# Window attention and two feed-forward layers on one core: one key tile for the first groups, a dummy exponential, a late `gcol`, and scores ahead of the preceding values

## The chip, the core and the metric

The kernel runs on one core of a Trainium2 chip. The metric is the device time of one execution in microseconds (us); each kernel is run several times and the median is compared. Lower is better.

The engines work side by side, each through its own list of instructions in order: PE (matmuls, turning by matmul), DVE (vector arithmetic), ACT (functions such as exp and tanh, and copies), POOL (slower vector arithmetic, and some transfers), SP (here it only issues transfers). A semaphore wait holds up the instruction that has it and all behind it on its engine.

## The reference

```python
# _attn_ref: q, k, v of (4, 8, 576, 64), causal, window of 64
scores = scale * np.matmul(q, k.transpose(0, 1, 3, 2))
mask = (rel >= 0) & (rel < window)
scores = np.where(mask, scores, -1000000000.0)
scores = scores - np.max(scores, axis=-1, keepdims=True)
attn = np.exp(scores)
attn = attn / (np.sum(attn, axis=-1, keepdims=True) + 1e-09)
return np.matmul(attn, v).astype(np.float32)
# _moe_ref: 2304 tokens, 512 -> 2048 -> 512
h = x @ w_in
g = h * (1.0 / (1.0 + np.exp(-1.702 * h)))
return (g @ w_out).astype(np.float32)
# _moe2_ref: 2304 tokens, 512 -> 1536 -> 512
rms = np.sqrt(np.mean(x * x, axis=-1, keepdims=True) + 1e-06)
xn = x / rms * rms_g
g = xn @ w_gate
silu = g * (1.0 / (1.0 + np.exp(-g)))
val = xn @ w_val
return (silu * val @ w_out).astype(np.float32)
```

The attention's output, as 2304 tokens of 512 values, is the input of the first feed-forward layer, and that layer's output the input of the second.

## The kernel before

**Groups.** The attention is cut into 36 groups of 64 tokens (`W`), all 8 heads of a group together. `attention(g, ...)` does one: scores on PE (into a PSUM bank), row maximum `nm` on DVE, exponentials with their sums `su` on ACT (four instructions a group), the reciprocals `rc` of the sums on DVE, the normalising product `e` by `rc` on POOL, the turning of `e` on PE, a copy of the turned probabilities to `pt` or `pts` on ACT or DVE, the values on PE, and then the result in two parts: `xh` (rounded, by ACT) and `xl` (the rest, by DVE). For the first 8 groups (`NS`) the mask is added by a matmul (`masked_scores`, L432 and L435), and the maximum is taken from PSUM (L440, L442); later groups use `scores`, `masked`, `highest`. From group 18 on (`NPE`) the turning is by DVE and 32 by 32 copies.

**Blocks.** The first layer works on six blocks of 512, 256, 384, 384, 384 and 384 tokens; `a_up` and `a_down` take one of 16 slices of `w_in` and `w_out` each: an up product is 12 matmuls (L554 to L556, three for each of four parts, the second of which reads `xl`), then tanh (L607) and gating (L611) into `th`, a split into `gh` and `gl`, and the down product (L628 to L630). The first block needs groups 0 to 7, the second 8 to 11, the third 12 to 17. The second layer (L912 to L914, L1013 to L1015) follows.

**Weights.** Weights come as 64-bit words of 512 KB for a slice. `w_narrow` loads one into a `raw` buffer (three of them, L336) and makes 32-bit numbers: one ACT step (L340), three DVE steps (L344, L348, L354). `w_split` cuts the number into a high half in a slab (ACT, L312) and a low half (L381, on POOL or DVE). During the first block all 32 slices go through this.

**Order.** Nothing is put in order by hand. Every step is entered with `pl.op(cost, ..., prio)`: costs for each engine that may do it, a priority, and the buffers that it reads, writes and takes. `Planner.emit` plays the steps through with these costs, always the ready one with the lowest priority number first, and the instructions of all engines are written in that order. A changed cost, priority or number of buffers can so move instructions anywhere behind it. `late` adds to the time after which the planner counts a step as finished.

**Start.** `load_q`, `load_k` and `load_v` load 256 KB each through SP. Keys are loaded as two windows at a time and the windows overlap, so each group's load repeats a window of the one before. Buffers: two `q` and four `q0`, two `k` and three `k0`, one `v` and three `v0`. The scores of the first 8 groups take PSUM banks `y0` to `y2` in turn. `gcol` (L1091, L1092) is the second layer's factor `rms_g`, halved; it is first read where the first block's results are scaled (L650, L653). `attention` is called with `step`, the distance by which turning and values come later in priority than scores.

Of the kernel before, what the change touches and what calls it, by code (L numbers as in the profile page):

```python
# [9 lines left out]
F32 = mybir.dt.float32  # L10
# [7 lines left out]
P = 128  # L18
# [188 lines left out]
def window_attention_two_moe_kernel(ctx: ExitStack, tc: tile.TileContext, ins, out):  # L207
# [74 lines left out]
        "q0": (start, 4, [P, NK, 2 * W], F32),  # L282
        "k0": (start, 3, [P, 2, NK, W], F32),
        "v0": (start, 3, [P, DM], F32),
# [7 lines left out]
    pts = at.tile([P, NK, P], F32, name="pts")  # L292

# [37 lines left out]
    def w_narrow(key, src, prio, after=(), apart=False, late=0.0):  # L331
# [25 lines left out]
        got = pl.op({"D": dma(P * 4096)}, fetch, prio - 3, new=[rb], after=after, late=late)  # L357
# [31 lines left out]
    q_of, kw, vw, vals = {}, {}, {}, []  # L389

# [9 lines left out]
    def load_k(g, prio, kind="k"):  # L400
# [3 lines left out]
        t = kw[b, i] = Buf(kind)  # L404
# [14 lines left out]
    def attention(g, p0, step, ekind="e", ptkind="pt", norm=("G",), ptev=("A", "V"), hi=("A",)):  # L419
        q, k, v = q_of.pop(g), kw[wkey(g)], vw[wkey(g)]  # L420
        sb, eb, nb, ub, rb = Buf(f"y{g % 3}" if g < NS else "abank"), Buf(ekind), Buf("nm"), Buf("su"), Buf("rc")
        tb, pb, ob = Buf("bank" if g < NS else "abank"), Buf(ptkind), Buf("abank")
        extra = [START] if ekind == "e0" or ptkind == "pt0" or q.kind == "q0" or k.kind == "k0" or v.kind == "v0" else []

        def scores(e):
            s = make(sb)
            for p in range(NK):
                nc.tensor.matmul(s[:, p * P:(p + 1) * P], q.tile[:, p], k.tile[:, :, p], start=True, stop=True)  # L428

        def masked_scores(e):  # L430
# [3 lines left out]
            for p in range(NK):  # L434
                nc.tensor.matmul(s[:, p * P:(p + 1) * P], q.tile[:, p], k.tile[:, :, p], start=False,  # L435
                                 stop=(p == NK - 1))
# [63 lines left out]
        if g < NS:  # L500
            pl.op({"T": 1.09}, masked_scores, p0, r=[q, k, "mask", "negative", "ident", *extra],
                  w=[("xh", c), ("xl", c), "scores order"], new=[sb])
            pl.op({"V": dve(512) + 0.1}, highest_of, p0, r=[sb], new=[nb])
            pl.op({"A": 4 * act(128, True, 2)}, powers_of, p0, r=[sb, nb, *extra], new=[ub, eb])
        else:
            pl.op({"T": 0.872}, scores, p0, r=[q, k, *extra], w=[("xh", c), ("xl", c), "scores order"], new=[sb, eb],
# [7 lines left out]
        if g < NPE:  # L514
            pl.op({"T": 0.436}, turned, p0 + d, r=[eb, "ident", *extra], w=["turned order"], new=[tb, pb])
# [20 lines left out]
        vals.append(pl.op({"T": 0.872}, values, p0 + d, r=[v, pb, "at", *extra] + (nov if g >= NPE else []), new=[ob]))  # L536
        cost = {"A": act(256, False), "V": dve(256)}
        pl.op({x: cost[x] for x in hi}, x_hi, p0 + d, r=[ob], w=[("xh", c)])
        pl.op({"V": dve(256)}, x_lo, p0 + d, r=[ob, ("xh", c)], w=[("xl", c)])
# [737 lines left out]
```

## Time and profile before

| | |
|---|---|
| median of 3 runs | 926.25 us (926.17 to 926.94) |
| span of the profiled execution | 923.7 us |
| PE busy | 902.2 us, 98% |
| DVE busy | 647.3 us, 70% |
| ACT busy | 438.4 us, 47% |
| POOL busy | 273.2 us, 30% |

The span runs from the first to the last instruction of the profiled execution; its own time with what lies around the span is not listed apart, and the runs' median is 2.55 us above it. Busy times are sums over stages with different limits: in the start no engine is busy throughout, in the first block DVE and PE both nearly are, later PE alone. So the stretches are read one by one, and in each the waits of the engine that is nearly full.

### The profile page before, as it was taken

The numbers are of one execution on the slowest core, as the hardware profiler recorded it, in microseconds if no ns is written. First come the engines' busy times: TensorE is split into PE (matmuls) and PEld (weight loads), VectorE is DVE, ScalarE is ACT, GpSimd is POOL, SyncE is SP. The second block draws the span as 40 slices with busy tenths as digits, with TensorE's granted clock in tenths as the row PEclk, the third lists the DMA queues.
The fourth block names the chain that finished last, engine by engine and source line by source line (L and its number), as shares of the span: only waits on it lengthen the run. The fifth ranks groups of instructions, "written<-read, shape, count | busy, mean of one in ns | idle before, by whom it ended". The sixth has DMA issues, their size and how long they took to land.

```text
span 923.7 us, 15362 instructions
## 1 busy us (share of the span) xinstructions
PE 902.2 (98%) x5436; PEld 835.9 (90%) x5436; DVE 647.3 (70%) x1236; ACT 438.4 (47%) x1081; POOL 273.2 (30%) x387
## 2 busy tenths in 40 slices
PE   8899999999999999999999999999999999999998
PEld 7677789989999999999998989898999999999997
DVE  5999996676767667666467888778667556555553
ACT  6666665566566667565336444443322223322222
POOL 4111012334345342442102622334223225222210
PEclk9999999999999999999999999999999999999999
DMA  8655557665445656543366999888986768966741
GB/s 283 226 174 201 193 188 159 222 206 171 151 147 186 169 183 229 183 160 114 106 231 233 234 359 341 320 280 255 321 236 206 206 201 244 284 205 205 205 144 68
DMA packets 86536, 194.63 MB, mean 211 GB/s; under 512 B 12726, under 2 KB 36027, under 8 KB 84924
## 3 DMA queue, kind: packets, MB, share of 16 engines
q1 hardware_dynamic: 66108, 137.02, 44.5%
q0 software_dynamic: 20352, 56.63, 21.0%
q8 instruction: 43, 0.70, 0.3%
q14 instruction: 33, 0.27, 0.1%
HBM read 140.13 MB, written 53.50 MB: 210 GB/s over the span
## 4 chain that ended last, share of the span: by engine, by line
PE 77%; DVE 12%; DMA 6%; issue 2%; ACT 2%; SPq 0%; POOL 0%; DVEq 0%; ACTq 0%; POOLq 0%
PE bank L912 9%; PE bank L913 9%; PE bank L914 9%; PE y L628 5%; PE y L630 5%; PE y L629 5%; PE bank L554 5%; PE bank L555 5%; PE bank L556 5%; PE y L1013 3%; PE y L1015 3%; PE y L1014 3%; PE abank L428 3%; DVE raw L348 2%; PE abank L487 2%
## 5 line engine op out<-in xcount | busy, mean ns | idle before, releaser
L554 PE MATMUL bank<-xh,slab 128*128 128x384 f32 (+2 forms) x288 | 98.3, 341 | 1.0 <-DVE th L611 1.0
L628 PE MATMUL y<-gh,slab 128*128 128x384 f32 (+2 forms) x288 | 98.5, 342 | 0.5 <-DVE y L653 0.5
L556 PE MATMUL bank<-xh,slab 128*128 128x384 f32 (+2 forms) x288 | 97.0, 337 | 2.0 <-DVE slab L381 2.0
L555 PE MATMUL bank<-xl,slab 128*128 128x384 f32 (+2 forms) x288 | 97.3, 338 | 0.4 <-DVE xl L494 0.3
L630 PE MATMUL y<-gh,slab 128*128 128x384 f32 (+2 forms) x288 | 96.9, 337 | 0.5 <-DVE slab L381 0.5
L629 PE MATMUL y<-gl,slab 128*128 128x384 f32 (+2 forms) x288 | 96.6, 336 | 0.0
L951 ACT ACTIVATE sb<-gh 128x384 f32<-128x384 f32 x72 | 37.8, 525 | 114.0 <-DVE gh L938 114.0
L312 ACT ACTIVATE xh<-sb 128x384 fp32r<-128x384 f32 x72 | 37.1, 521 | 107.5 <-DVE sb L966 107.5
L938 DVE TENSOR_TENSOR gh<-gl,bank 128x384 f32<-128x384 f32 x108 | 59.3, 551 | 35.9 <-PE bank L914 35.1
L611 DVE SCALAR_TENSOR_TENSOR th<-th,bank 128x384 f32<-128x384 f32 (+2 forms) x96 | 52.7, 549 | 42.8 <-ACT th L607 42.3
L913 PE MATMUL bank<-slab,late 128*128 128x384 f32 x228 | 77.0, 338 | 0.0
L913 PE MATMUL bank<-slab,slab 128*128 128x384 f32 x228 | 76.4, 335 | 0.0
L607 ACT ACTIVATE th<-bank 128x384 f32<-128x384 f32 (+2 forms) x96 | 46.7, 486 | 58.1 <-PE bank L556 55.0
L472 POOL TENSOR_TENSOR e<-e,rc 128x512 f32<-128x512 f32 x34 | 37.8, 1111 | 108.9 <-DVE rc L469 102.8
L312 ACT ACTIVATE gh<-th 128x384 fp32r<-128x384 f32 (+2 forms) x96 | 50.2, 523 | 40.3 <-DVE th L611 31.3
L938 DVE TENSOR_TENSOR gl<-gl,bank 128x384 f32<-128x384 f32 x72 | 39.8, 553 | 35.4 <-PE bank L914 31.4
L463 ACT ACTIVATE e<-e,nm 128x128 f32<-128x128 f32 x112 | 43.7, 393 | 33.2 <-DVE nm L458 31.0
L556 PEld LDWEIGHTS bank<-xh,slab 128*128 128x128 f32 x288 | 54.1, 188 | 4.9 <-DVE slab L381 2.8
L554 PEld LDWEIGHTS bank<-xh,slab 128*128 128x128 f32 x288 | 54.1, 188 | 3.6 <-DVE th L611 1.6
L630 PEld LDWEIGHTS y<-gh,slab 128*128 128x128 f32 x288 | 54.1, 188 | 3.2 <-DVE slab L381 1.2
L555 PEld LDWEIGHTS bank<-xl,slab 128*128 128x128 f32 x288 | 54.1, 188 | 3.1 <-DVE xl L494 1.1
L912 PE MATMUL bank<-slab,slab 128*128 128x384 f32 x156 | 53.0, 340 | 3.8 <-ACT th L312 1.7
(198 smaller groups left out, 2596.9 us busy)
## 6 DMA issues: line engine op xcount, KB each, us to landing
slab<-wc POOLq DMA_DIRECT2D x36, 512.0 KB, 4.6
late<-wc POOLq DMA_DIRECT2D x36, 512.0 KB, 4.3
wp<-raw SPq DMA_DIRECT2D x24, 512.0 KB, 4.1
fw<-wp SPq DMA_DIRECT2D x12, 1024.0 KB, 8.1
late<-wo POOLq DMA_DIRECT2D x22, 512.0 KB, 5.5
q<-in_q_dram SPq DMA_DIRECT2D x36, 256.0 KB, 4.4
wc<-slab SPq DMA_DIRECT2D x18, 512.0 KB, 7.1
wc<-late SPq DMA_DIRECT2D x18, 512.0 KB, 5.7
```

The lines of the kernel that those rows point to most:

```text
L312: nc.scalar.activation(out=out, in_=in_, func=AF.Copy)
L554: nc.tensor.matmul(h, w[:, 0, kk], xh_ring[:, kk, cols], start=(kk == 0), stop=False)
L555: nc.tensor.matmul(h, w[:, 0, kk], xl_ring[:, kk, cols], start=False, stop=False)
L556: nc.tensor.matmul(h, w[:, 1, kk], xh_ring[:, kk, cols], start=False, stop=(kk == NK - 1))
L611: nc.vector.scalar_tensor_tensor(out=th, in0=th, scalar=1.0, in1=hb.tile[:, 0:n], op0=ALU.add, op1=ALU.mult)
L628: nc.tensor.matmul(y, s[:, 0, cols], hb.tile[:, 0:n], start=first, stop=False)
L629: nc.tensor.matmul(y, s[:, 0, cols], lb.tile[:, 0:n], start=False, stop=False)
L630: nc.tensor.matmul(y, s[:, 1, cols], hb.tile[:, 0:n], start=False, stop=last)
L912: nc.tensor.matmul(h, w[:, 0, kk], xh[:, kk], start=kk == 0, stop=False)
L913: nc.tensor.matmul(h, w[:, 0, kk], xl[:, kk], start=False, stop=False)
L914: nc.tensor.matmul(h, w[:, 1, kk], xh[:, kk], start=False, stop=kk == 1)
L938: nc.vector.tensor_tensor(out=(make(to) if kind else s.tile)[:, 0:HT].bitcast(F32), in0=s.tile[:, 0:HT].bitcast(F32), in1=b.tile[:, 0:HT], ...
```

## The change

- Keys of the first groups: one tile `k_start` of six windows is filled by three loads of two windows; groups 0 to 5 read it. A group's keys are now a function that gives the tile's part (`k()`), with the list of its load steps beside it (`ktok`), a window pair across two loads having two. The `k0` buffers are gone.
- `q0` has two buffers instead of four, `v0` five instead of three. The loads of the first 8 groups are written as one list with priorities in that order.
- A dummy exponential of one column (`first_exp`) stands first on ACT.
- `gcol` is loaded with priority 1 instead of -20 and scaled with priority 14 instead of 0.
- The first weight's load has a lead of 20.8 instead of 3.0.
- `attention` takes a separate step for the values, `vstep`. For the first 8 groups both stay 0.5; for the later ones turning has 1.7 and values 2.5, where both had 2.
- Costs of scores, turning, values and exponentials in the planner are other numbers.

```diff
-        "q0": (start, 4, [P, NK, 2 * W], F32),
-        "k0": (start, 3, [P, 2, NK, W], F32),
-        "v0": (start, 3, [P, DM], F32),
+        "q0": (start, 2, [P, NK, 2 * W], F32),
+        "v0": (start, 5, [P, DM], F32),
...
+    KS = 6
+    k_start = start.tile([P, KS, NK, W], F32, name="k_start")
...
-        got = pl.op({"D": dma(P * 4096)}, fetch, prio - 3, new=[rb], after=after, late=late)
+        got = pl.op({"D": dma(P * 4096)}, fetch, prio - lead, new=[rb], after=after, late=late)
...
-    def attention(g, p0, step, ekind="e", ptkind="pt", norm=("G",), ptev=("A", "V"), hi=("A",)):
-        q, k, v = q_of.pop(g), kw[wkey(g)], vw[wkey(g)]
+    def attention(g, p0, step, vstep, ekind="e", ptkind="pt", norm=("G",), ptev=("A", "V"), hi=("A",)):
+        q, (k, ktok), v = q_of.pop(g), kw[wkey(g)], vw[wkey(g)]
+        qk = [q, *ktok]
...
-            pl.op({"T": 1.09}, masked_scores, p0, r=[q, k, "mask", "negative", "ident", *extra],
+            pl.op({"T": 1.2}, masked_scores, p0, r=[*qk, "mask", "negative", "ident", *extra],
...
-            pl.op({"A": 4 * act(128, True, 2)}, powers_of, p0, r=[sb, nb, *extra], new=[ub, eb])
+            pl.op({"A": 1.4}, powers_of, p0, r=[sb, nb, *extra], new=[ub, eb])
...
-        vals.append(pl.op({"T": 0.872}, values, p0 + d, r=[v, pb, "at", *extra] + (nov if g >= NPE else []), new=[ob]))
+        vals.append(pl.op({"T": 0.65}, values, p0 + vstep, r=[v, pb, "at", *extra] + (nov if g >= NPE else []), new=[ob]))
...
+    first_exp = start.tile([P, 1], F32, name="first_exp")
     pl.op({"V": 0.2}, lambda e: nc.vector.memset(warm, 0.0), -99, w=["warm"])
+    pl.op({"A": 1.4}, lambda e: nc.scalar.activation(out=first_exp, in_=warm[:, 0:1], func=AF.Exp), -99, r=["warm"])
...
+    for i in range(KS - 1):
+        kw[0, i] = (lambda i=i: k_start[:, i:i + 2]), starts[i // 2:(i + 1) // 2 + 1]
+    loads = [(load_k_start, 0), (load_q, 0, "q0"), (load_q, 1, "q0"), (load_k_start, 2), (load_q, 2), (load_v, 0),
+             (load_q, 3), (load_k_start, 4), (load_q, 4, "q0"), (load_v, 2, "v0"), (load_q, 5, "q0"), (load_k, 6),
+             (load_q, 6), (load_v, 3, "v0"), (load_k, 7), (load_q, 7)]
+    loads += [(load_v, g, "v0") for g in range(4, NS)]
+    for n, (fn, g, *kind) in enumerate(loads):
+        fn(g, n - 95, *kind)
...
-    pl.op({"D": 0.45}, lambda e: nc.sync.dma_start(out=gcol, in_=rms_g), -20, w=["gcol"])
+    pl.op({"D": 0.45}, lambda e: nc.sync.dma_start(out=gcol, in_=rms_g), 1, w=["gcol"], late=6.0)
     pl.op({"V": 0.1}, lambda e: nc.vector.tensor_scalar(out=gcol, in0=gcol, scalar1=0.5, scalar2=None, op0=ALU.mult),
-          0, w=["gcol"])
+          14, w=["gcol"])
...
-        w_narrow(key, src, prio)
+        w_narrow(key, src, prio, lead=3.0 if i else 20.8)
...
-            attention(g, p - 0.3, 2)
+            attention(g, p - 0.3, 1.7, 2.5)
```

How this moves instructions, in three places. Line numbers of the changed kernel are some 4 to 14 higher.

First, DVE where the last of the first 8 groups are under way (`xl` is a group's low part, `pts` and `pt` the copies of turned probabilities, `raw` a weight being narrowed). Before:

```order
L494 TENSOR_TENSOR xl<-abank,xh 128x4x64
L1092 TENSOR_SCALAR gcol<-gcol 128x4
L314 COPY pts<-bank 128x512
L344 TENSOR_SCALAR raw<-raw 128x512
L314 COPY pt_546<-bank 128x512
L348 SCALAR_TENSOR_TENSOR raw<-raw 128x512
```

Now:

```order
L498 TENSOR_TENSOR xl<-abank,xh 128x4x64
L349 SCALAR_TENSOR_TENSOR raw<-raw 128x512
L355 SCALAR_TENSOR_TENSOR raw<-raw 128x512
L472 TENSOR_SCALAR rc<-su 128x4
L473 RECIPROCAL rc<-rc 128x4
L315 COPY pts<-bank 128x512
```

`gcol` no longer stands ahead of the copies; the first weight's steps stand between the `xl` parts.

Second, DVE at the ninth group, behind the reciprocals of its sums; with them POOL starts the normalising product. Before:

```order
L468 TENSOR_SCALAR rc<-su 128x4
L469 RECIPROCAL rc<-rc 128x4
L381 TENSOR_TENSOR slab_86<-raw,slab_86 128x512
L611 SCALAR_TENSOR_TENSOR th<-th,bank 128x512
L381 TENSOR_TENSOR slab_83<-raw,slab_83 128x512
```

Now:

```order
L472 TENSOR_SCALAR rc<-su 128x4
L473 RECIPROCAL rc<-rc 128x4
L615 SCALAR_TENSOR_TENSOR th<-th,bank 128x512 x2
L345 TENSOR_SCALAR raw<-raw 128x512
L573 TENSOR_TENSOR gl<-th,gh 128x512
```

The two low halves of weights behind the reciprocals have gone to POOL, and the gating stands there.

Third, PE where the second block ends and the third begins with `slab_82` (`ident,e` is the turning of a group, `pts,v` the values, `k,q` the scores of the next group, `late_...` the second block's last slices). Before:

```order
L477 MATMUL abank<-ident,e 128x128 x4
L628 MATMUL y_1690<-gh,late_1310 128x256
L629 MATMUL y_1690<-gl,late_1310 128x256
L630 MATMUL y_1690<-gh,late_1310 128x256
L487 MATMUL abank<-pts,v 64x64 x8
L428 MATMUL abank<-k,q 128x128 x4
L554 MATMUL bank<-xh,slab_82 128x384
L555 MATMUL bank<-xl,slab_82 128x384
```

Now:

```order
L634 MATMUL y_1692<-gh,late_1299 128x256
L491 MATMUL abank<-pts,v 64x64 x8
L558 MATMUL bank<-xh,late_1304 128x256
...
L634 MATMUL y_1692<-gh,late_1301 128x256
L432 MATMUL abank<-k,q 128x128 x4
L558 MATMUL bank<-xh,slab_82 128x384
L559 MATMUL bank<-xl,slab_82 128x384
```

The last values of the third block's groups now have an up product and a down product of the second block behind them, ahead of the third block's first product.

## Rows read from the trace of the kernel before

**Rows 1.** The page, busy us, share and instructions of each engine:

```profile
PE 902.2 (98%) x5436; PEld 835.9 (90%) x5436; DVE 647.3 (70%) x1236; ACT 438.4 (47%) x1081; POOL 273.2 (30%) x387
```

**Rows 2.** By stretch: length, busy PE, PEld, DVE, ACT, POOL, clock, DMA share, GB/s:

```profile
5.77:32.00 26.23, 20.78 (x232) 17.49 (x231) 20.16 (x56) 20.42 (x82) 7.42 (x8) 0.93 0.88 292
32.00:150.00 118.00, 114.12 (x629) 92.64 (x630) 110.74 (x197) 75.26 (x161) 18.56 (x16) 1.00 0.55 187
150.00:200.00 50.00, 48.80 (x446) 46.68 (x444) 32.37 (x70) 27.99 (x93) 12.38 (x14) 1.00 0.70 196
```

**Rows 3.** PE's waits, whole span: us in total, times, longest:

```profile
PE abank L487 <- DVE pts L314: 2.8, 1, 2.8
PE bank L556 <- DVE slab L381: 2.0, 2, 1.3
...
PE y L432 <- ACT e L448: 1.1, 1, 1.1
...
PE bank L912 <- DVE th L611: 1.0, 1, 1.0
...
PE y L630 <- DVE slab L381: 0.5, 1, 0.5
```

**Rows 4.** Timeline of ACT at the first group: start, length, instruction, idle before:

```profile
6.75 1.28 ACT L448 ACT_TABLE_LOAD   x1 [6.75 <-DVE nm L442]
8.04 0.37 ACT L448 ACTIVATE e<-y,nm 128x128 f32<-128x128 f32 x1
...
9.43 0.38 ACT L448 ACTIVATE t<-y,nm 128x128 f32<-128x128 f32 x1
```

**Rows 5.** Timeline around `gcol`, all engines:

```profile
17.26 0.44 SPq L1091 DMA_DIRECT2D gcol<-in_rms_g_dram  x1
...
23.50 0.17 DVE L1092 TENSOR_SCALAR gcol<-gcol 128x4 f32<-128x4 f32 x1 [1.54 <-DMA gcol<-in_rms_g_dram]
23.57 0.68 DVE L314 COPY pts<-bank 128x512 f32<-128x512 f32 x1
...
24.31 0.83 PE L487 MATMUL abank<-pts,v 128*64 128x64 f32 x16 [2.79 <-DVE pts L314]
...
25.07 1.12 PE L477 MATMUL bank<-ident,e 128*128 128x128 f32 x4
```

**Rows 6.** Two microseconds after it, by stretch:

```profile
26.00:28.00 2.00, 1.78 (x26) 1.45 (x27) 1.97 (x7) 1.77 (x4) 0.00 (x0) 0.50 0.84 266
```

**Rows 7.** DVE's groups, 5.7 to 32 us: busy, mean ns, idle before:

```profile
L440 DVE TENSOR_REDUCE nm<-y 128x4 f32<-128x512 f32 x8 | 5.5, 683 | 2.5 <-PE y L435 2.4
...
L468 DVE TENSOR_SCALAR rc<-su 128x4 f32<-128x4 f32 x8 | 1.4, 171 | 2.5 <-ACT e L448 1.3 <-ACT t L448 1.0
...
L381 DVE TENSOR_TENSOR slab<-raw,slab 128x512 fp32r<-128x512 f32 x1 | 0.7, 686 | 0.0
```

**Rows 8.** Timeline at the first up product:

```profile
31.58 0.42 DVE L494 TENSOR_TENSOR xl<-abank,xh 128x256 fp32r<-128x256 f32 x1
...
32.06 0.50 PE L555 MATMUL bank<-xl,slab 128*128 128x512 f32 x1 [0.32 <-DVE xl L494]
```

**Rows 9.** Timeline in the first block, POOL, DVE and PE:

```profile
77.13 1.31 POOL L472 TENSOR_TENSOR e<-e,rc 128x512 f32<-128x512 f32 x1 [3.15 <-DVE rc L469]
...
77.46 1.53 DVE L381 TENSOR_TENSOR slab<-raw,slab 128x512 fp32r<-128x512 f32 x1
...
79.04 0.50 PE L556 MATMUL bank<-xh,slab 128*128 128x512 f32 x1 [1.34 <-DVE slab L381]
```

**Rows 10.** Timeline of PE where the third block begins, the four waits:

```profile
191.11 0.38 PE L629 MATMUL y<-gl,late 128*128 128x256 f32 x1 [0.48 <-POOL gl L569]
...
192.56 0.66 PE L477 MATMUL abank<-ident,e 128*128 128x128 f32 x4 [0.26 <-POOL e L472]
...
193.97 0.69 PE L487 MATMUL abank<-pts,v 128*64 128x64 f32 x16 [0.39 <-ACT pts L312]
...
200.78 0.44 PE L554 MATMUL bank<-xh,slab 128*128 128x384 f32 x1 [0.55 <-DVE th L611]
```

More of the change, by code (lines that the diff above doesn't have):

```diff
@@ L329, in window_attention_two_moe_kernel, with w_narrow @@
     w32 = {}
-    def w_narrow(key, src, prio, after=(), apart=False, late=0.0):
+    def w_narrow(key, src, prio, after=(), apart=False, late=0.0, lead=3.0):
         rb = Buf("raw")
@@ L389, in window_attention_two_moe_kernel @@
     q_of, kw, vw, vals = {}, {}, {}, []
+    starts = [("keys", n) for n in range(KS // 2)]
     def wkey(g):
@@ L403, in load_k @@
         b, i = wkey(g)
-        t = kw[b, i] = Buf(kind)
+        t = Buf(kind)
+        kw[b, i] = (lambda: t.tile), [t]
         pl.op({"D": dma(P * 2048)}, lambda e: nc.sync.dma_start(out=make(t), in_=kh[b, :, i:i + 2]), prio, new=[t])
@@ L427, in scores @@
             for p in range(NK):
-                nc.tensor.matmul(s[:, p * P:(p + 1) * P], q.tile[:, p], k.tile[:, :, p], start=True, stop=True)
+                nc.tensor.matmul(s[:, p * P:(p + 1) * P], q.tile[:, p], k()[:, :, p], start=True, stop=True)
         def masked_scores(e):
@@ L434, in masked_scores @@
             for p in range(NK):
-                nc.tensor.matmul(s[:, p * P:(p + 1) * P], q.tile[:, p], k.tile[:, :, p], start=False,
+                nc.tensor.matmul(s[:, p * P:(p + 1) * P], q.tile[:, p], k()[:, :, p], start=False,
                                  stop=(p == NK - 1))
@@ L514, in attention @@
         if g < NPE:
-            pl.op({"T": 0.436}, turned, p0 + d, r=[eb, "ident", *extra], w=["turned order"], new=[tb, pb])
+            pl.op({"T": 0.4}, turned, p0 + d, r=[eb, "ident", *extra], w=["turned order"], new=[tb, pb])
             cost = {"A": act(512, False), "V": dve(512)}
@@ L1081, in window_attention_two_moe_kernel, with load_k_start @@
     pl.op({"G": 0.1}, lambda e: nc.gpsimd.memset(mhalf, -0.5), -97, w=["mhalf"])
[L1083 to L1089 removed]
+    def load_k_start(i, prio):
+        tok = starts[i // 2]
+        pl.op({"D": dma(P * 2048)}, lambda e: nc.sync.dma_start(out=k_start[:, i:i + 2], in_=kh[0, :, i:i + 2]), prio, w=[tok])
+    for i in range(KS - 1):
[6 more added lines that the diff above has]
+        fn(g, n - 95, *kind)
+    for g in range(NS):
+        attention(g, -60 + g, 0.5, 0.5, "e0" if g >= 2 else ("e", "t1")[g], "pt0" if g % 2 else "pt",
                   norm=("G",) if g < NS - 1 else ("V",))
[L1091 removed]
+    pl.op({"D": 0.45}, lambda e: nc.sync.dma_start(out=gcol, in_=rms_g), 1, w=["gcol"], late=6.0)
     pl.op({"V": 0.1}, lambda e: nc.vector.tensor_scalar(out=gcol, in0=gcol, scalar1=0.5, scalar2=None, op0=ALU.mult),
[L1093 removed]
+          14, w=["gcol"])
     pl.op({"V": 0.2}, lambda e: nc.vector.tensor_scalar(out=ones, in0=ident, scalar1=0.0, scalar2=1.0,
```

14 lines of the change are left out of this document (4 added, 10 removed).

## The prediction

> **What bounds the kernel now.** I read the page's busy times first: PE, the matmul engine, is busy for 902 of 923.7 us [rows 1]. So nothing that the change does to other engines counts unless it fills one of PE's gaps, and all gaps together are some 21 us: that is the ceiling, 2.3%. The table by stretch then says where they lie [rows 2]: of the 26.2 us from the first row maximum on DVE (5.77) to the last part of the first token block (32.0), PE works 20.8 and DVE, the vector engine, only 20.2; in the next 118 us, the first block's feed-forward layer, PE is idle for 3.9 and DVE is busy for 110.7 of 118, so these two are nearly balanced there; from 150 to 200 us PE is idle for 1.2. The list of PE's waits names the reasons [rows 3]: one wait of 2.8 us for a copy of turned probabilities, two for a weight's low half (2.0), one for the exponentials (1.1), one for a `th` tile where the second layer begins (1.0).
>
> The three rows that the change aims at are these. ACT, the activation engine, loads its function table at 6.75, 1.28 us long, between the first group's maximum and its first exponential, and then does one group each 1.39 us (8.04 to 9.43) [rows 4]. The dummy exponential asks for the same table at the start, where ACT has nothing to do until 6.75, so it costs nothing itself. DVE stands still for 1.54 us at 23.50, because the scaling of `gcol` waits for a 2 KB transfer that was issued at 17.26 behind the weights; the copy of the turned probabilities is queued behind it, and PE waits 2.79 us for that copy [rows 5]. [...] The first layer's first matmul chain cannot go past its second matmul before the last `xl` part is written: it is issued at 31.58 and the matmul follows at 32.06 after 0.32 of waiting [rows 8]. The time of this last `xl` is therefore the measure of the whole start.
>
> **The change part by part: the start.** DVE writes that last `xl`, and it is the engine to count. Before, it does 20.16 us of work in 26.23, so it is idle for 6.07 [rows 2]. The changed order gives DVE nearly the same list up to the eighth `xl`: one copy of turned probabilities more (0.68 [rows 5], since ACT does one fewer), one low half of a weight less (0.69 [rows 7], it goes to POOL) and no `gcol` (0.17). The work stays at 20.0 us and only idle time can be won. It has four parts [rows 5, 7]: 1.5 for `gcol`; 2.5 before the sums' reciprocals (L468), for ACT; 2.4 before the row maxima, of which 1.4 lie ahead of 5.77; and some 1.0 for the smaller ones. The first goes altogether: `gcol`, which is not read until the first block's results are scaled, is now prepared some twenty-five DVE instructions after the last of the eight `xl`, and its transfer is issued after the loads of the ninth and tenth group, so the copy is no longer behind it. Of the second I take 1.8 (the 1.0 of the second group, whose exponentials start 1.28 us earlier with the table already loaded, and 0.8 of the 1.3 that the other groups wait). Of the waits for the scores I take nothing: the first scores still wait for masks and identity. So 1.5 + 1.8 = 3.3 us.
>
> Bounds for this term: the lower one is the `gcol` wait alone, 1.5; the upper one adds all of L468's 2.5 and 0.5 for matmuls that ran at the low clock (the turning's 1.12 us [rows 5]), 4.5. Whether the clock falls again I cannot exclude: PE still has gaps of about a microsecond between the last groups.
>
> The table load is 1.28 us in the row and the exponential follows at once (8.04) [rows 4]. [...]
>
> The loads. The key tile holds six windows in three transfers, where five were made before, so two transfers of 256 KB fall away in the first eight groups. With five value buffers the values no longer wait for the matmuls of earlier groups, while only two query buffers are left beside the two that stay; the fifth and sixth group's queries wait for the first two groups' scores, which are long done. Ahead of the first weight stand 17 transfers of 256 KB now; with the weight they are 5.0 MB, and at the 292 GB/s of this stretch [rows 2] they need 17 us, so the weight lands at about 19. DVE comes to it at about that time by my count. I cost this at nothing, and at 1 us where it is late; it is inside the lower bound.
>
> **The first block, 32 to 150 us.** The head start is worth something only if it is not used up here. Two things speak for that. Up to the point where the first block's results are scaled, the changed order gives DVE four low halves of weights fewer (0.69 each [rows 7]) and two narrowing steps of a weight of the second layer fewer, together some 3.5 us of 110; the low halves go to POOL, which works for 18.6 of 118 us [rows 2]. And the largest waits there have one cause: POOL normalises a group's probabilities (77.13, 1.31 us), DVE's low half of a weight starts beside it and takes 1.53 instead of 0.69, and PE waits 1.34 [rows 7, 9]. In the order before, such a low half comes right behind or one instruction behind the reciprocals of four groups; in the changed order two of the four have other work there that did not suffer in the trace, and for two (the eleventh and twelfth group) it is the same. I take one of PE's three waits for them as won, the shortest, 0.5 us [rows 3]. Bounds: a gain of 2.5, all three, and a loss of 1.3, one more wait as long as the longest.
>
> [...]
>
> **The later groups, 150 to 200 us and on.** With values at +2.5 and turning at +1.4 instead of both at +1.7 of a plan step, PE's order ahead of the third block changes: before it is turning, a quarter of a down product, values, scores, the new block's first product; now whole products stand between turning, values and scores, and two of the old block's down products come after the new block's first product. PE waits at this place four times: 0.48, 0.26, 0.39, 0.55 [rows 10], together 1.7. With whole products between them, the first three have cover; I take 1.3, bounds 0 and 1.7. Between 200 and 500 us there is nothing of this kind to win: PE is busy throughout. The second layer's matmuls keep their order to the end; the 1.0 at its beginning [rows 3] I leave, with 1.0 either way, since other engines' work is dealt out anew.
>
> **Sum.** 3.3 + 0.5 + 1.3 = 5.1 us off the profiled span of 923.7, so 918.6. The median of the runs, 926.25, lies 2.55 above that span, and I take this as constant: 921.15, said as 921.2.
>
> **The rivals.** First, only `gcol` is won at the start: the exponentials come sooner, but the scores' arrival or the first weight then sets DVE's pace. For it: DVE already waits for scores, 2.4 us [rows 7]. Against it: the fourth group's scores waited for exponentials, not for data [rows 3]. Then 1.5 + 0.5 + 1.3 = 3.3, 922.95: still faster.
>
> Second, the head start is handed back in the first block, because DVE and the weights' buffers set the pace there and not PE. For it: 110.7 of 118 us of DVE work. Against it: PE's 3.9 us of idleness is as small, and DVE has less to do. Only the boundary's 1.3 stays: 924.95, no change.
>
> Third, on the other side: POOL's low halves become the late ones. Ten of the first layer's low halves are on POOL in the changed order and six before, and each is some 0.6 us longer than on DVE. If a product waits 1.3 us for each, as the longest wait for a slab [rows 3], seven of ten cost 9.1; less 3.3 and 1.3 that is 4.5 us slower, 930.75. It decides from the fifth on: four such waits cost 5.2, 0.6 more than the 4.6 won, and five cost 6.5, which is slower by more than 0.2%. Against it: no wait of PE for a slab in the trace names POOL, all name DVE.
>
> Fourth, nearly all upper bounds are met, 4.5 + 2.5 + 1.7 and half of the second layer's 1.0: 9.2 us, 917.0.
>
> **How the numbers follow.** A measurement of this kernel can tell some 0.2%, 1.85 us, from no change: faster is below 924.4, slower above 928.1. Chances: forecast 0.58, first rival 0.13, second 0.14, third 0.09, fourth 0.06. Faster 0.58 + 0.13 + 0.06 = 0.77, same 0.14, slower 0.09. The range must reach the first, second and fourth: 917.0 to 925.2 leaves out the third and about a tenth spread over the ends of the others.
>
> **What would show it.** Right: no idle time of DVE before `gcol`; the table load in the first 3 us; the eighth `xl` at about 28.7 and the first product right behind; PE's waits for a slab at 2 us or less in 32 to 150; no more than 0.5 us of waits where the third block begins. Wrong: a first product later than 30.5 (first rival), PE idle for 6 us or more in the 118 us behind it (second), waits of PE for POOL's slabs (third), or a longer stretch at the low clock than before 28 us.

## The result: one per cent slower, and the profile after

| | before | after |
|---|---|---|
| median of the runs, us | 926.21 (923.99 to 926.94, 6 runs) | 936.20 (933.21 to 938.05, 6 runs) |
| profiled span, us | 923.7 | 933.7 |
| ratio after to before | | 1.010, 95% interval 1.0081 to 1.0119 |

The change makes the kernel 10 us slower. The forecast, 921.2 us with a range of 917.0 to 925.2, was on the wrong side of no change. The line of the page with the busy times answers to [rows 1]:

```profile
PE 907.3 (97%) x5436; PEld 839.8 (90%) x5436; DVE 646.9 (69%) x1237; ACT 435.2 (47%) x1071; POOL 273.8 (29%) x397
```

PE has as many instructions as before. It is busy for 5.1 us more, some 2 us of it by the clock (mean granted clock 0.995 against 0.997), and idle for 4.9 us more. The table by stretch says where it lies (columns as in [rows 2]):

```profile
5.77:32.00 26.23, 22.38 (x240) 19.57 (x240) 23.17 (x58) 20.10 (x82) 9.25 (x9) 0.90 0.82 289
32.00:150.00 118.00, 115.99 (x637) 93.56 (x637) 103.59 (x191) 77.88 (x169) 24.32 (x21) 0.99 0.55 182
150.00:200.00 50.00, 46.19 (x421) 45.18 (x421) 27.11 (x63) 24.08 (x79) 11.30 (x13) 0.97 0.65 172
200.00:500.00 300.00, 294.21 (x1941) 287.60 (x1940) 199.07 (x379) 165.77 (x466) 96.37 (x170) 1.00 0.53 167
```

The first two stretches became better, as forecast: PE idles for 3.9 instead of 5.5 us and for 2.0 instead of 3.9. A part of this is only that matmuls at the lower clock take longer (it is 0.50 from 26.72 to 33.54 us, and the last scores take 2.08 us in it; at 1.00, in a run below, 1.16): by equal work (below) the changed kernel is 0.2 us ahead at 33.0 and 0.7 at 155.2. From 150 to 200 us it idles for 3.8 instead of 1.2, and from 200 to 500 us for 5.8; the same stretch of the kernel before is this row, with 1.6:

```profile
200.00:500.00 300.00, 298.41 (x1964) 291.71 (x1963) 194.12 (x372) 173.44 (x477) 106.88 (x171) 1.00 0.51 171
```

The list of PE's waits over the whole span (us in total, times, longest) has at its head:

```profile
PE abank L491 <- DMA v<-in_v_dram: 9.1, 4, 3.8
PE bank L916 <- ACT th L313: 2.9, 3, 1.7
```

L491 is the values' matmul (L487 before). PE stands and waits for the load of `v`, 9.1 us in four places. In the kernel before no wait for that load is longer than 0.2 us. Of the second row, 1.7 us in one wait stood in the kernel before as well. The wait of 2.8 us for the copy `pts` at the head of [rows 3] is gone; before the same values PE now stands for 1.56 us, and the profile names no releaser:

```profile
25.28 0.69 PE L491 MATMUL abank<-pts,v 128*64 128x64 f32 x16 [1.56 <-issue]
```

The timeline has the three long waits for `v`, ahead of 165, 233 and 403 us (start, length, instruction, idle before):

```profile
165.41 0.69 PE L491 MATMUL abank<-pts,v 128*64 128x64 f32 x16 [3.81 <-DMA v<-in_v_dram]
232.79 0.77 PE L491 MATMUL abank<-pts,v 128*64 128x64 f32 x16 [2.89 <-DMA v<-in_v_dram]
402.86 0.78 PE L491 MATMUL abank<-pts,v 128*64 128x64 f32 x16 [2.14 <-DMA v<-in_v_dram]
```

What keeps a load of 256 KB so long? SP's timeline ahead of the first of them, first of after, then of before:

```profile
154.45 0.33 SPq L416 DMA_DIRECT2D v<-in_v_dram  x1
154.83 0.43 SPq L704 DMA_DIRECT2D rs<-ss  x1
155.31 0.50 SPq L400 DMA_DIRECT2D q<-in_q_dram  x1
```

```profile
152.34 0.38 SPq L700 DMA_DIRECT2D rs<-ss  x1
157.40 0.33 SPq L413 DMA_DIRECT2D v<-in_v_dram  x1
```

`rs<-ss` writes the reciprocal roots of a block's norms, 2 KB in all, to DRAM. Its layout "(t p) -> p (one t)" puts neighbouring values into different partitions, so it goes in 512 pieces of 4 bytes. Before, the load of `v` was issued 5 us after it; now it is issued 0.4 us ahead of it, and the values want it some 7 us later. Stretches of 2 us of after (columns as above; the last three are clock, DMA share and GB/s):

```profile
154.00:156.00 2.00, 2.00 (x28) 1.93 (x25) 1.61 (x3) 0.98 (x4) 0.65 (x1) 1.00 0.78 258
...
158.00:160.00 2.00, 2.00 (x20) 2.00 (x18) 0.80 (x2) 0.42 (x1) 0.68 (x1) 1.00 0.89 45
160.00:162.00 2.00, 1.59 (x15) 1.40 (x13) 0.72 (x2) 1.28 (x3) 0.28 (x1) 1.00 1.18 33
162.00:164.00 2.00, 0.00 (x0) 0.00 (x0) 1.08 (x2) 0.00 (x0) 0.45 (x1) 1.00 0.41 23
164.00:166.00 2.00, 0.59 (x16) 0.58 (x16) 0.00 (x0) 0.00 (x0) 0.00 (x0) 1.00 0.78 75
166.00:168.00 2.00, 2.00 (x14) 1.98 (x12) 0.76 (x2) 1.87 (x10) 0.00 (x0) 0.67 0.92 234
168.00:170.00 2.00, 2.00 (x12) 2.00 (x11) 0.35 (x2) 0.61 (x2) 1.04 (x1) 0.50 0.79 304
```

From 158 to 162 us the DMA engines are as busy as ever (0.89, 1.18) and move 33 to 45 GB/s instead of 258. By the packets in the trace it is not the pieces of 4 bytes that are busy: they take 9 ns each (median), and nearly all begin between 155 and 159 us. Packets of 2 KB, of the loads around them, took up to 6.8 us, where 0.08 is the median: the small writes are out, and what is beside them does not get on. PE has nothing to do from 162 to 164, and pays twice: when it goes on, its granted clock falls to 0.50 (from 166.66 to 170.07 us). The kernel before had the same stretch, and it could have been read there:

```profile
156.00:158.00 2.00, 2.00 (x29) 1.80 (x28) 0.60 (x2) 0.98 (x3) 0.00 (x0) 1.00 0.94 16
```

0.94 busy, 16 GB/s. Only nobody on PE waited: the next values came at 165.88, 8.5 us after the load.

The second long wait has its load of `v`, issued at 222.63, 3.9 us behind the second write. Again little is moved there, though loads of `q` and `k` went out at 219.89 and 220.29, but this time at a low DMA share:

```profile
220.00:222.00 2.00, 2.00 (x16) 1.75 (x16) 1.97 (x4) 1.41 (x5) 0.86 (x3) 1.00 0.04 16
```

The third comes by a detour. Behind the fourth write, issued at 377.95, two transfers `wp<-raw`, issued at 381.81 and 383.35, need some 10 us each; SP stands for 8.6 us until they are done (in e1, below, for 2.7) and issues the load of `v` only then, behind three of weights. The chain that ended last has both (start, length):

```profile
383.35 10.40 DMA wp<-raw
395.60 7.12 DMA v<-in_v_dram
```

To follow gains and losses along the kernel, I gave each matmul of the trace a fixed length by its form, added these up, and compared the times at which two kernels have done the same amount. Differences to the kernel before in us (minus is ahead), at its own times in the first column:

```
before   after  e12   e4    e1    e2    e5    e6    e8
 25.6    -2.9  -3.8  -0.9  -3.2   0.1  -1.1  -2.6  -2.6   ahead of the first product
 33.0    -0.2  -3.5  -0.5  -0.2   0.5   1.2  -0.1  -0.1
155.2    -0.7  -3.8   2.7  -1.1   0.8   2.3   0.2   0.0   end of the first block
171.0     4.4   3.1   9.8  -1.4   0.8   2.1   0.2   0.0   first wait for v
215.6     1.3  -0.1   7.4  -4.6   1.7  -1.0  -0.2  -3.2   third block begun
256.7     4.7   6.0  14.8  -4.3   1.7  -0.6  -0.2  -2.9   second wait for v
411.3     7.4  13.1  25.9  -4.3   1.7   0.3   0.6  -0.7   a later wait for v
472.0     7.4  13.1  26.0  -4.4   1.7   0.4   1.2  -0.8
546.9    10.9  12.4  28.2  -7.1   0.7  -2.2  -0.7  -1.8   second layer begun
918.3    10.3  11.9  27.7  -7.6   0.7  -2.7  -1.3  -2.4   end
```

The columns behind the first are experiments, below: e12 is the change with that write on another queue, e4 the later groups' steps alone, e1 the change with larger pieces, e2 the kernel before with larger pieces, e5 and e6 the two halves of the change with larger pieces, e8 is e1 with `gcol` early. These are single profiled executions, so a difference of a microsecond between two columns says little. Where the new order has put other matmuls first, the fixed lengths matter too: other lengths move the rows 256.7 and 411.3 by up to 1.6 us, 155.2 and 171.0 by up to 0.9, and the others by 0.3 or less.

### The profile page after: what moved, and what is told of

It reads as the page before. It is cut to its first block, busy times and chain, and to the rows that moved or that the text cites. A ratio compares the mean times of both kernels' runs of the same rounds, so it can differ in the third digit from the quotient of the medians.

```text
span 933.7 us, 15359 instructions
## 1 busy us (share of the span) xinstructions
PE 907.3 (97%) x5436; PEld 839.8 (90%) x5436; DVE 646.9 (69%) x1237; ACT 435.2 (47%) x1071; POOL 273.8 (29%) x397
## 2 busy tenths in 40 slices
DMA packets 86248, 194.11 MB, mean 208 GB/s; under 512 B 12694, under 2 KB 35995, under 8 KB 84636
## 4 chain that ended last, share of the span: by engine, by line
PE 78%; DMA 9%; DVE 7%; ACT 3%; issue 2%; SPq 1%; POOL 0%; DVEq 0%; ACTq 0%; POOLq 0%
PE bank L916 9%; PE bank L917 8%; PE bank L918 8%; PE bank L558 5%; PE y L632 5%; PE bank L560 5%; PE bank L559 5%; PE y L634 5%; PE y L633 5%; PE y L1017 3%; PE y L1019 3%; PE y L1018 3%; DMA v<-in_v_dram 3%; PE abank L432 2%; PE abank L491 2%; DMA words<-xn 2%
## 5 line engine op out<-in xcount | busy, mean ns | idle before, releaser
L632 PE MATMUL y<-gh,slab 128*128 128x384 f32 (+2 forms) x288 | 100.6, 349 | 0.1
L558 PE MATMUL bank<-xh,slab 128*128 128x384 f32 (+2 forms) x288 | 99.7, 346 | 0.0
L634 PE MATMUL y<-gh,slab 128*128 128x384 f32 (+2 forms) x288 | 97.6, 339 | 0.9 <-POOL slab L382 0.7
L560 PE MATMUL bank<-xh,slab 128*128 128x384 f32 (+2 forms) x288 | 98.0, 340 | 0.0
L573 DVE TENSOR_TENSOR gl<-th,gh 128x384 fp32r<-128x384 f32 (+2 forms) x76 | 47.2, 622 | 24.3 <-ACT gh L313 24.1
L634 PEld LDWEIGHTS y<-gh,slab 128*128 128x128 f32 x288 | 54.5, 189 | 4.4 <-DVE slab L382 1.5
L632 PEld LDWEIGHTS y<-gh,slab 128*128 128x128 f32 x288 | 54.4, 189 | 4.3 <-ACT y L654 0.6
```

The lines of the kernel that those rows point to most:

```text
L558: nc.tensor.matmul(h, w[:, 0, kk], xh_ring[:, kk, cols], start=(kk == 0), stop=False)
L560: nc.tensor.matmul(h, w[:, 1, kk], xh_ring[:, kk, cols], start=False, stop=(kk == NK - 1))
L632: nc.tensor.matmul(y, s[:, 0, cols], hb.tile[:, 0:n], start=first, stop=False)
L634: nc.tensor.matmul(y, s[:, 1, cols], hb.tile[:, 0:n], start=False, stop=last)
```

## The experiments

**Larger pieces, nothing else moved (e1_rows, e2_before_rows).** Both ends of the norms' way through DRAM get the layout in which a partition's values are neighbours. The order of instructions on every engine stays as it was; 256 to 512 pieces of 4 bytes become 128 of 8 to 16 bytes (the page of after counts 12694 packets under 512 B, that of e1 9622).

```diff
-in_=ms_d[j].rearrange("one (t p) -> p (one t)", p=P)
+in_=ms_d[j].rearrange("one (p t) -> p (one t)", p=P)
-nc.sync.dma_start(out=rs_d[j].rearrange("one (t p) -> p (one t)", p=P), ...
+nc.sync.dma_start(out=rs_d[j].rearrange("one (p t) -> p (one t)", p=P), ...
```

> The changed kernel in which the two small transfers of the first layer's norm take neighbouring words per partition: ss from ms and rs from ss move pieces of 8 to 16 bytes, 128 of them, instead of 256 to 512 pieces of 4 bytes; the order of all instructions is the same and the result too. Theory A (the 4-byte pieces hold up every transfer issued behind them for some 8 us, and the values' loads now stand there): PE's waits of 3.8 and 2.9 us for v at 165 and 233 us fall under 0.5, the low clock after the first one goes (1.7), the 2.1 at 403 stays: 927 to 929. Theory B (the one v buffer is freed too late, and a load of 256 KB needs its 5 us whatever is ahead): the waits stay at over 1.5 each: 933 to 936.

> The kernel before with the same two transfers in neighbouring words. Theory A: its values' loads are issued 5 us or more behind the small pieces and are hardly held up, so 924 to 926.5, no change or a little faster. If other waits hang on the pieces as well, 922 or less.

Measured: e1 917.96 us (ratio to the kernel before 0.989, 0.9871 to 0.991), e2 925.65 (0.9973, 0.9962 to 0.9984). So the changed order with larger pieces is faster than both kernels. The pieces cost the kernel before some 2 us and the changed one 18. The load of `v` is issued as before, right ahead of `rs<-ss`, and the values follow without a wait, in the timeline of e1:

```profile
153.99 0.33 SPq L416 DMA_DIRECT2D v<-in_v_dram  x1
154.38 0.42 SPq L704 DMA_DIRECT2D rs<-ss  x1
```

```profile
161.06 0.69 PE L491 MATMUL abank<-pts,v 128*64 128x64 f32 x16
```

The same 2 us as above now move 292 GB/s:

```profile
158.00:160.00 2.00, 2.00 (x20) 2.00 (x19) 0.43 (x1) 0.47 (x2) 0.23 (x1) 1.00 0.83 292
```

A load of `v` takes 3.4 us to land (median), a write of 1 KB 4.9; the same two rows of after say 4.9 and 8.7. From the list of DMA issues (KB each, us to landing) of e1:

```profile
v<-in_v_dram SPq DMA_DIRECT2D x32, 256.0 KB, 3.4
rs<-ss SPq DMA_DIRECT2D x1, 1.0 KB, 4.9
```

and of after:

```profile
v<-in_v_dram SPq DMA_DIRECT2D x32, 256.0 KB, 4.9
rs<-ss SPq DMA_DIRECT2D x1, 1.0 KB, 8.7
```

The loss beyond the waits for `v` goes too: at 546.9 us e1 is 7.1 ahead and the changed kernel 10.9 behind. I had expected 927 to 929, with the smaller waits staying; the pieces carry the whole loss and more.

**The two halves of the change, with the small pieces (e3_later_undone, e4_later_alone).** e3 sets the later groups' steps back and keeps the start; e4 puts the new steps into the kernel before.

```diff
 # e3, on the changed kernel
-attention(g, p - 0.3, 1.7, 2.5)
+attention(g, p - 0.3, 2, 2)
 # e4, on the kernel before
-attention(g, p - 0.3, 2)
+attention(g, p - 0.3, 1.7, 2.5)
```

> The changed kernel with turning and values of the later groups both at 2 again, so the start, gcol, the loads and the costs alone. If the later groups' steps are the cause: waits for v under 0.5 us in total, 925 to 927 (the start itself is worth 1 us). If the start's change upsets the plan: 930 or more.

> The kernel before with only the later groups' turning at 1.7 and values at 2.5. If these steps are the cause, waits of PE for v of 5 us or more in total and 932 to 938. If they cost only together with the new start or costs: 925 to 928.

(In e4 `attention` takes the second step as in the changed kernel.) Measured: e3 928.15 (1.0001, 0.9986 to 1.0016), e4 953.51 (1.0276, 1.0257 to 1.0295). The loss belongs to the later groups' steps: without them there is none (e3 was expected at 925 to 927), alone they cost 26 us, more than twice what I expected. The pieces still cost e3 something: it waits 1.3 us for `v` in two places, and with larger pieces (e6, below) its ratio is 0.9956. PE's waits in e4:

```profile
PE abank L487 <- DMA v<-in_v_dram: 20.0, 5, 6.0
```

The clock adds its part: it falls within the wait that ends at 172.35, 5.80 us long (mean granted clock 0.94 from 166 to 169 us, 0.50 from 169 to 173), and over the work behind the wait, from 173 to 176 us, its mean is 0.59:

```profile
173.00:176.00 3.00, 3.00 (x24) 2.88 (x21) 0.42 (x1) 0.95 (x2) 0.09 (x1) 0.59 0.48 111
```

What the order costs depends on where the loads fall beside the six norm writes; the start moves these places, so the whole change lost less than its one half.

**The two halves with larger pieces (e5_later_rows, e6_start_rows).** The edits of e4 and e3, each with that of e1.

> The kernel before with two things of it changed: the later groups' steps 1.7 and 2.5 (as the kernel with the later steps alone, which took 953.5 us) and the two small norm transfers in pieces of 8 to 16 bytes. Theory A (the values behind the next scores cost time only through the loads of v that queue behind the 4-byte pieces): all of the 26 us above the kernel before goes, and PE's waits for v fall from 20.0 us in 5 to under 1.5 us: 922 to 927 us. Theory B (one buffer for v that comes free later is too late by itself, whatever the pieces): a third to a half of the loss stays, 932 to 945, with waits for v of 2 us and more still there.

> The changed kernel with the later groups' steps back at 2 and the small norm transfers in pieces of 8 to 16 bytes: the change of the first eight groups and of gcol alone, without the pieces. If the gain of the changed kernel with larger pieces (918.0) comes from the start and the third block's boundary, this one shows it too: 918 to 921. If the order of the later groups carries part of it, this one stays behind by that part: 921 to 925.

Measured, with the neighbours in one table:

| with larger pieces | median us | ratio to the kernel before |
|---|---|---|
| kernel before (e2) | 925.65 | 0.9973 (0.9962 to 0.9984) |
| and the later groups' steps (e5) | 923.91 | 0.9966 (0.9952 to 0.998) |
| and the start with `gcol` (e6) | 922.79 | 0.9956 (0.9941 to 0.9971) |
| and both (e1) | 917.96 | 0.989 (0.9871 to 0.991) |

With larger pieces the steps that cost e4 26 us cost nothing (the largest wait for `v` is 0.2 us). So the order alone is no loss; theory B falls. The lines of equal work show what each half brings: e5 wins 3.1 us between 171.0 and 215.6, where the third block begins, e6 next to nothing (0.4) there; e6 is 2.6 us ahead before the first product and has lost that at 33.0. Both together win more than the sum of the two, by 0.6% or some 5 us. Part of it is that e5's profiled execution lost 2.3 us to the lower clock between 25.6 and 33.0, which e2 did not; the rest is not explained by these runs.

**Write or read (e10_rs_only).** Only the write `rs<-ss` gets larger pieces.

> The changed kernel with larger pieces for the transfer from ss to rs alone (the write); the read from ms to ss stays at 4 bytes, so norms are given to other columns (the output is not the reference's; no step is left out). If the writes of 4 bytes hold up the loads of v behind them: waits for v under 1 us and 917 to 920. If the reads do, which come some 2 us ahead of the writes: 931 to 936. If both: 922 to 930.

Measured: 919.73 (0.9913, 0.988 to 0.9946), no wait for `v` above 0.2 us. The writes of 4 bytes do it. What the reads, still at 4 bytes, cost beside them is not shown: the medians of e10 and e1 lie 1.8 us apart, and the intervals of these two overlap.

**Another queue (e12_rs_pool_queue).** The changed kernel with its 4-byte pieces, `rs<-ss` issued by GpSimd.

```diff
-nc.sync.dma_start(out=rs_d[j].rearrange("one (t p) -> p (one t)", p=P), ...
+nc.gpsimd.dma_start(out=rs_d[j].rearrange("one (t p) -> p (one t)", p=P), ...
```

> The changed kernel with the write from ss to rs, still in pieces of 4 bytes, issued from GpSimd's queue instead of SyncE's; nothing else. Theory Q (the load of v waits because it stands behind those pieces in one queue): the waits for v go, as with larger pieces: 918 to 922. Theory E (the 4-byte writes hold the DMA engines themselves or the memory behind them, whatever queue they come from): the waits for v stay at 9 us in 3 or near it, 931 to 938; GpSimd's own work for the issue could add up to 2 us to either.

Measured: 937.81 (1.0105, 1.0074 to 1.0135), as slow as the change itself:

```profile
PE abank L491 <- DMA v<-in_v_dram: 11.5, 3, 5.2
```

Its timeline on SP and POOL, and on PE:

```profile
151.31 0.33 SPq L416 DMA_DIRECT2D v<-in_v_dram  x1
151.46 0.97 POOL L704 DMA_DIRECT2D rs<-ss  x1
```

```profile
163.66 1.12 PE L491 MATMUL abank<-pts,v 128*64 128x64 f32 x16 [5.21 <-DMA v<-in_v_dram]
```

The load that the values at 163.66 need is the one issued 0.15 us ahead of the write, for `v` has one buffer and its next load is issued only at 164.81; it came 12 us later. So it is not the order inside SP's queue: the write holds up a load of another queue, and PE waits 5.21 us for it. On GpSimd's queue the trace lists a write of 2 KB as 16 packets of 128 bytes (the page of e12 counts 10486 packets under 512 B, that of after 12694), so what the two runs share is the layout in DRAM, in places of 4 bytes, and not the packets; a write in the other layout from this queue was not run. Whether the load stands in the DMA engines or in the memory behind them no run here tells.

**The clock at the start (e7_filler, e9_filler_small).** In the changed kernel the granted clock is at 0.50 from about 26.7 to 33.5 us. On top of e1, matmuls whose result nothing reads fill PE's gaps between the last of the first groups: 32 in e7, nine in e9.

```diff
+def filler(n):
+    t = make(Buf("y3"))
+    for i in range(n):
+        nc.tensor.matmul(t[:, 0:P], warm, warm, start=True, stop=True)
 # in turned(), behind the last transpose
+if NS - 2 <= g < NS:
+    filler(8)        # e9: filler(10 - g)
 # in values(), behind the last matmul
+if NS - 4 <= g < NS:  # e9: if g == NS - 2
+    filler(4)        # e9: filler(2)
```

> The changed kernel with larger pieces, and 8 matmuls of 128x128 into an unused bank behind the turnings of the last two of the first 8 groups and 4 behind the values of the last four, which compute nothing that is read. Theory C (the clock that is at half from 26 to 33 us eats the start's gain, since PE idles between the groups' last steps): the granted clock stays at full there and the first block, some 3.3 us of work less than it took, ends earlier: 914.5 to 916.5. Theory D (the clock follows what came before or is not moved by so little): still at half for as long, 917.5 to 919.5, the fillers adding up to 0.7.

> The changed kernel with larger pieces, and nine matmuls of 128x128 whose result nothing reads (4 behind the turning of group 6, 2 behind its values, 3 behind the turning of group 7): about 2.4 us of PE work into the 2.9 us that PE idles there between 23 and 28 us. If the half clock from 26 to 33 us comes from those idle stretches and eats the start's gain, the clock stays full, the last scores and the first products take half as long there, and the kernel takes 915 to 917. If the clock falls all the same, or the fillers stand in the way of the values: 918 to 920.

Measured: e7 924.96 (0.9975, 0.9961 to 0.9989), e9 919.1 (0.9904, 0.9867 to 0.9941). Two stretches of e1, then of e9:

```profile
24.00:27.00 3.00, 1.54 (x20) 1.29 (x20) 3.00 (x8) 2.11 (x6) 1.30 (x1) 0.85 0.44 147
27.00:31.00 4.00, 3.31 (x27) 2.97 (x26) 3.31 (x7) 2.52 (x5) 0.00 (x0) 0.50 0.68 248
```

```profile
24.00:27.00 3.00, 2.35 (x30) 2.23 (x30) 3.00 (x8) 2.28 (x6) 1.12 (x1) 1.00 0.53 160
27.00:31.00 4.00, 3.98 (x35) 3.40 (x35) 3.97 (x9) 2.40 (x5) 0.43 (x1) 1.00 0.91 288
```

With fillers the clock stays at 1.00 in both, and over all executions its mean is 0.999 or 1.000 in e7 and 1.000 in e9, where e1 has 0.996 in three of four. e7 put some 8 us of filler on PE (eight of the 32 matmuls took 1.95 us), far more than the gaps hold, and loses by its own weight, outside both ranges that I had expected: its first product is at 33.91. e9 fits into the gaps and begins the first block 2 us earlier than e1:

```profile
28.65 0.48 PE L567 MATMUL bank<-xh,slab 128*128 128x512 f32 x1
```

Yet it ends where e1 does. By equal work without the fillers e9 is 3.2 us ahead of the kernel before at 33.0 and 0.8 at 155.2: handed back in the first block, in waits of the turning for POOL's product `e`, 2.8 us against 1.0 in e1:

```profile
PE abank L486 <- POOL e L481: 2.8, 3, 1.3
```

e12 has the changed kernel's order at the start without fillers, its clock did not fall, and it kept 3.8 us to the end of the first block. So the clock varies between executions of one order; why e9, with the fillers in its order, hands its gain back is not shown. What the fall costs at the end can be read from the runs of one kernel: in e1 the execution at a mean clock of 1.000 took 917.57 us and the three at 0.996 took 917.96 to 919.17; in e6 those at 0.999 and 1.000 took 922.44 and 921.99, those at 0.996 took 923.13 and 923.87. By these few it is some 1 us.

**Single parts of the start (e8_gcol_early, e11_no_first_exp).** On top of e1, `gcol` is loaded and scaled early as before (e8), or the dummy exponential is left out (e11).

```diff
 # e8
-pl.op({"D": 0.45}, lambda e: nc.sync.dma_start(out=gcol, in_=rms_g), 1, w=["gcol"], late=6.0)
+pl.op({"D": 0.45}, lambda e: nc.sync.dma_start(out=gcol, in_=rms_g), -20, w=["gcol"])
...
-          14, w=["gcol"])
+          0, w=["gcol"])
 # e11
-pl.op({"A": 1.4}, lambda e: nc.scalar.activation(out=first_exp, in_=warm[:, 0:1], func=AF.Exp), -99, r=["warm"])
```

> The changed kernel with larger pieces and gcol loaded and halved early, as in the kernel before. In the prediction gcol was worth 1.5 us on DVE; by that 919 to 920. If DVE had no time to spare for it in the denser start and the planner's order behind it falls back too (the third block's boundary), up to 922. If gcol's wait hides in other idle time: 917.5 to 918.5.

> The changed kernel with larger pieces without the dummy exponential, so that the first exponential loads the table as in the kernel before. The prediction took 1.8 us for DVE's waits for ACT at the start, of which the table load is 1.28 us. If that reaches the first product and stays: 919 to 920. If the half clock at the start eats it: 917.5 to 918.8.

Measured: e8 919.94 (0.9917, 0.9899 to 0.9935), e11 919.48 (0.9908, 0.9876 to 0.9939). The medians lie 2.0 and 1.5 us above e1, the sizes that the prediction gave these parts, but the intervals overlap with that of e1 (0.9871 to 0.991), so neither is shown by the times. By equal work e11 is 1.2 us behind e1 at 25.6 and 1.6 at the end; e8 is 0.6 behind at 25.6 and most of its 5 us at the end come later.

## Why the prediction was wrong, step by step

**The bound.** PE is what counts; that held, in both directions: the 10 us are PE's, 4.9 of them idle.

**The start, 3.3 us (1.5 to 4.5).** The changed kernel was 2.9 us ahead at 25.6, up to the last group. `gcol` waits no more; the table load stands at the front, and the first exponential at 7.71 finds it done:

```profile
0.73 1.28 ACT L1069 ACT_TABLE_LOAD   x1 [0.73 <-PEq L1280]
```

But the first row maximum came at 6.71 instead of 5.77, so the first exponential is only 0.33 us earlier, not 1.28. That is not the order's doing: the start of before has the first maximum at 5.77 and, in e2, at 7.01, the changed start between 5.68 (e9) and 7.01 (e8). In the changed start all that follows moves with it: e12, e1, the changed kernel and e8 have it at 5.79, 6.43, 6.71 and 7.01 and are 3.8, 3.2, 2.9 and 2.6 us ahead at 25.6. So e8, with `gcol` early, has lost nothing there, and its scaling of `gcol` at 23.86 waits for nothing: the 1.5 us of this wait were won, but in this order the late place of `gcol` was not needed for it. e11, at 6.30, is 1.3 us behind this line, the length of the table load. Of the other terms, DVE's waits before the sums' reciprocals fell from 2.5 to 0.7 us, the 1.8 of the forecast, while DVE's work up to the eighth `xl` was 21.1 us and not 20.0; 1.0 more is in the short `nm` steps (last section).

The eighth `xl` came at 29.51 and the first product at 30.71, where 28.7 was forecast; this is the sign that the prediction named for its failure, together with the longer stretch at the lower clock. The last scores at that clock took 2.08 us, in e12, at a clock of 1.00, 1.16:

```profile
28.98 2.08 PE L432 MATMUL abank<-k,q 128*128 128x128 f32 x8
30.71 0.77 PE L558 MATMUL bank<-xh,slab 128*128 128x512 f32 x1
```

In e12 the first product is at 28.35 (and its eighth `xl` at 28.09). Its first maximum is where it was before (5.79 against 5.77), and at 33.0 it is 3.5 us ahead. So the forecast of 3.3 and of 28.7 was good for the order and wrong for the clock:

```profile
28.35 0.48 PE L558 MATMUL bank<-xh,slab 128*128 128x512 f32 x1
```

The clock of before was at 0.50 from 26 to 28 us [rows 6], and the prediction wrote that it could not exclude another fall, but gave it no price in the sum and none in the lower bound. Between these two executions of one order lie 3.3 us at 33.0; 0.9 of them were there at 25.6, by the first maximum, so the fall cost 2.4. It came at 26.72, behind a stretch at 1.00; why in one of two executions of one order and not in the other is not shown.

**The first block, 0.5 us (-1.3 to 2.5).** PE's waits for weight slabs between 28 and 150 us fell from 2.5 us to 1.0, so the step was right and within its bounds; POOL works 24.3 us where it worked 18.6, and PE waits for its slabs 0.7 us, once. The third rival, which feared that, did not come true. Start and block together were 3.8 in the forecast; measured at 155.2: 0.7 in the changed kernel, 1.1 in e1, 3.8 in e12.

**The third block's beginning, 1.3 us (0 to 1.7).** Right in mechanism, too small: 3.1 us between 171.0 and 215.6 in the changed kernel, 3.2 in e1, 3.1 in e5, 0.4 in e6. None of the four waits of [rows 10] is left. The term counted only the waits that the timeline prints, 1.7 of the 1.75 us that PE is idle there before. The rest shows in the weight loads, not in PE's idle time: from 171.0 to 215.6 us they stand still for 4.0 us before, and for 0.8 in the same part of the changed kernel.

**The later groups, nothing: the step that failed.** The prediction wrote "Between 200 and 500 us there is nothing of this kind to win: PE is busy throughout", and counted the new steps as a change of PE's order alone. The value buffers it weighed only for the first eight groups, which have five. The later groups have one. Values that stand behind the next group's scores free it at another place, and the load that waits for it is issued there, beside the norms' writes, which held up a load beside them for some 8 us (7.5 in after and 8.9 in e12, by the numbers of the last section). That cost 5.1 us between 155.2 and 171.0 (3.8 of wait and the low clock behind it), 6.1 between 215.6 and 472.0 (5.3 of them in three waits for `v`) and 3.5 where the second layer begins; less the 3.1 of the third block, 0.7 from the start and 0.6 at the end these are the 10.3 of the profile. Of the 3.5 us at the second layer the waits name `gl`, `th` and `gh` of DVE and ACT, not the loads; e1 wins 2.7 there instead, so the pieces are behind them too. For 2.2 of them the trace has the way: the sixth write is issued at 533.00, and 6 us later SP stands in a single issue for 4.85 us, which takes 0.42 before and in e1:

```profile
539.07 4.85 SPq L902 DMA_DIRECT2D y<-wr  x1
```

From there the chain that ended last runs over a load `wc<-slab` of 4.90 us and DVE's steps to PE's wait of 1.24 us for `gl` at 554.17. The other 1.3 us were not followed.

None of the rivals was of this kind, though its signs stood in the trace before: `v` has one buffer, a stretch at 0.94 DMA share with 16 GB/s lay right in front of the values, and SP's order showed the load of `v` moving from two places behind the first `rs<-ss` to the place ahead of it. Had "who waits behind the moved instruction" been asked for its buffer too, and not only for its engine, this rival would have stood there.

## What to carry to other kernels

When an instruction is moved later, ask which buffer it frees, which transfer waits for that buffer, and what that transfer will now be issued beside: on a single-buffered load, the distance from the last reader to the next is the whole budget. Look for stretches that move few GB/s although loads have been issued, at a high DMA share (0.89 and 1.18 behind the first write) or a low one (0.04 behind the second); here they stood behind a transfer in tiny pieces. Every load that is wanted soon after (here some 7 us behind its issue, and PE waited 3.81 for it) has to be kept away from it, or better, the pieces made larger: a change of two layouts turned 1.0% slower into 1.1% faster. And price a fall of the clock as a term with a chance, not as a remark: at the start it took 2.4 of 3.5 us in one execution and nothing in another.

## What the runs showed of the hardware

- A write of 2 KB from SBUF to DRAM, into 512 places of 4 bytes, held up a load issued beside it: the values that wait for it began 10.9 us behind its issue (after) and 12.3 (e12), where a load lands after 3.4 (e1, median), whether the write came from the load's queue or another. 128 writes of 16 bytes did not (e1: the values began 7.1 us behind the load's issue, without a wait for it). With reads of 4 bytes left (e10) no wait for `v` above 0.2 us stayed.
- PE's granted clock fell to 0.50 at 166.66 behind a wait of PE of 3.81 us (up to 165.41, after) and within one of 5.80 us (up to 172.35, e4). At the start it fell to 0.50 in the profiled executions of after (26.72 to 33.54 us) and e1 (0.50 from 27 to 31) and stayed at 1.00 in that of e12, with one order and, from 20 us up to the fall, the same gaps between the same matmuls (0.25, 1.56 or 1.57, and 0.45 or 0.46 us); with nine small matmuls in the gaps its mean was 1.000 in all four executions of e9.
- DVE's scaling of 128x4 elements (L446), 0.17 us alone, took 0.6 us beside POOL's product of 128x512 in four of the eight groups of the start (in the kernel before in one), each time until 0.03 us or less behind the end of that product (here 10.83):

```profile
8.56 0.17 DVE L446 TENSOR_SCALAR nm<-nm 128x4 f32<-128x4 f32 x1
9.79 1.04 POOL L476 TENSOR_TENSOR e<-e,rc 128x512 f32<-128x512 f32 x1 [5.81 <-DVE rc L473]
10.25 0.61 DVE L446 TENSOR_SCALAR nm<-nm 128x4 f32<-128x4 f32 x1
```
